# Rest-row query transposes in one group, W_out blocks fetched one product earlier in strip 0, and one tile's transposes later

## The chip, the cores and the metric

The kernel runs on one core of a Trainium2 chip. The metric is the device time of one execution in microseconds (us). Lower is better.

## The reference

Attention without softmax comes first, and a two-layer network on its output follows. All data are float32 in the kernel; the two weight matrices reach it as 64-bit floats and are converted on the chip.

```python
kv  = einsum('bhsd,bhse->bhde', k, v)      # q, k, v: 8 batches, 8 heads, 576 rows, 64 columns
out = einsum('bhsd,bhde->bhse', q, kv)
out = out / sqrt(mean(out*out, -1) + 1e-6) * g_norm
x   = out.transpose(0, 2, 1, 3).reshape(4608, 512)
h   = x @ w_in                             # 512 x 2048
y   = maximum(h, 0)**2 @ w_out             # 2048 x 512
```

## The kernel before

**Tiles and strips.** The 4608 rows of x form 36 tiles of 128 rows. Four tiles make a strip, so there are nine strips, 0 to 8. A batch has 576 = 4 x 128 + 64 rows. The 64 left over are the "rest" rows; those of an even batch and of the odd one after it share a tile (`k_rest`, `v_rest`, `q_rest`), so that two batches give nine tiles. Tile 8 is the last of batches 0 and 1, and the first that belongs to strip 2.

**Attention slices.** Attention is cut into a list `slices`. For each batch b and each pair of heads p there is `transposed_query(b, p)` and `key_value(b, p)`; after the four pairs of a batch come `query` and `normalized` for two tiles at a time, and a function that brings the normalized tile into the transposed form `xT` that the network needs: `features` (transposes on TensorE) for tiles of batches 0 and 1, `squares_x` (VectorE and DMA) afterwards. `attend(n)` runs the list up to place n. The main loop calls it between the products of the network, so the network's matmuls and attention share TensorE in one fixed order.

**Queries of batches 0 and 1.** They are transposed on TensorE into PSUM tile `t_ps` (L339) and copied out by ScalarE (L341). For odd b, that is b = 1 here, each pair of heads also transposes its part of `q_rest` (L345, PSUM tile `tr_ps`) and copies it (L348). `t_ps`, `kv_ps` of `key_value` (L357, copied by L359 and L360) and `xt_ps` of `features` (L475) take turns in two PSUM places (tag `at`, `bufs=2`). `tr_ps` uses the place of the query products `x_ps` (tag `x`, one place).

**Strip 0.** The up-products (L614) run while the weights are still being converted: ScalarE does L210 and L213 on a raw piece, VectorE L222 to L231, and SyncE loads the next piece into a freed place (L198). The down-products of strip 0 use one level of a Strassen-like scheme with seven products, in the order 1, 2, 5, 6, 7, 3, 4, each of 32 matmuls in two halves (L578). Products 1, 2 and 5 find their blocks of W_out in `w_in`'s place. Products 6, 7, 3 and 4 fetch theirs from a DRAM copy (`w_out`) with `stream()` into `w_blk` tiles.

**Blocks and their sums.** During the first half of each of the seven products VectorE also makes four sums of the product's block (`deep_sums`, 128 x 2048 in all, tile `w_t`). They are written to DRAM (`w_deep`, L698) for the later strips, which use two levels of the scheme (L768). `w_blk` and `w_t` share four places (tag `w_blk`). A new tile takes a place that has been freed and waits for the last use of it.

**Order.** Every engine executes its instructions in the order in which the program records them, and nothing is reordered by a scheduler. SyncE issues nearly all DMAs, so a DMA that waits holds the ones recorded behind it. `load_rest(2)` and `load_q_rest(2)` load the rest rows of batch 2; the second is eight small DMAs (L162). `sums_in(g)` (L257, L259, L248) scales and sums W_in's blocks for the later strips, and `sums_x(1)` makes four sums of strip 1's x for its products 5, 6, 7 and 4.

Of the kernel before, what the change touches and what calls it, by code (L numbers as in the profile page):

```python
# [10 lines left out]
FP32 = mybir.dt.float32  # L11
# [9 lines left out]
def kernel(  # L21
# [225 lines left out]
    def minus(eng, out, a, b):  # L247
        eng.tensor_tensor(out=out, in0=a, in1=b, op=ALU.subtract)  # L248
# [71 lines left out]
    def open_rest(b):  # L320
        t = qt_pool.tile([P, NP, P], FP32, name="qT_rest", tag="qT_rest", bufs=1)
        for p in range(NP):
            qT["rest", b // 2, p] = t[:, p]
        return t

    def transposed_query(b, p):
        t = main.pop(("q", b, p))
        if b >= Q_ON_PE:
            qT[b, p] = qt_pool.tile([P, C, P], FP32, name="qT", tag="qT")
            nc.vector.transpose(out=flat(qT[b, p]), in_=flat(t))  # L330
            if b % 2 and p == NP - 1:
                nc.vector.transpose(
                    out=open_rest(b).rearrange("p q (k t) -> p q k t", k=4),
                    in_=squares(q_rest[b // 2]).rearrange("p k q f -> p q k f"),
                )
            return
        ps = apsum.tile([P, C, P], FP32, name="t_ps", tag="at")
        for c in range(C):
            nc.tensor.transpose(ps[:, c, :], flat(t[:, c]), ident)  # L339
        qT[b, p] = qt_pool.tile([P, C, P], FP32, name="qT", tag="qT")  # L340
        nc.scalar.copy(qT[b, p], ps)  # L341
        if b % 2:
            t = q_rest[b // 2][:, 2 * p : 2 * p + 2]
            ps = apsum.tile([P, 2, C * P], FP32, name="tr_ps", tag="x", bufs=1)[:, 0, 0:P]
            nc.tensor.transpose(ps, flat(t), ident)  # L345
            if p == 0:
                open_rest(b)
            nc.scalar.copy(qT["rest", b // 2, p], ps)  # L348

    def key_value(b, p):  # L350
        tk, tv = main.pop(("k", b, p)), main.pop(("v", b, p))
# [168 lines left out]
    for b in range(1, B):  # L520
        for p in range(NP):
            slices += [(transposed_query, (b, p)), (key_value, (b, p))]
        first_n = b // 2 * PAIR + (C if b % 2 else 0)
        ns = list(range(first_n, first_n + C + b % 2))
        for i in range(0, len(ns), 2):
            slices += [(query, (ns[i : i + 2],)), (normalized, (ns[i : i + 2],))]
            for n in ns[i : i + 2]:
                slices.append((features if b < X_ON_PE else squares_x, (n,)))
                if n % NT == NT - 1:
                    ready[n // NT] = len(slices)  # L530
    slice_at = [0]

    def attend(n):
        while slice_at[0] < min(n, len(slices)):
            fn, a = slices[slice_at[0]]
            fn(*a)
            slice_at[0] += 1
# [115 lines left out]
    to_stream += [(s, p, n) for s in range(DEEP, N_STRIP) for p in DEEP_ORDER for n in range(2)]  # L653
    to_stream = iter(to_stream)

    def stream(n=1):
        for _, u in zip(range(n), to_stream):
            p = u[1]
            t = stream_pool.tile([P, 4, FQ // 2, P], FP32, name="w_blk", tag="w_blk")
            if len(u) == 2:  # L660
                w_blk[u] = t.rearrange("p (h a) f e -> p h (a f) e", h=2)
                nc.sync.dma_start(out=w_blk[u], in_=w_out[B_OUT[p]])
            elif u[2] == 0:

                nc.sync.dma_start(
                    out=t[:, 1:4], in_=w_out[B_OUT[p]].rearrange("p h (a f) e -> p (h a) f e", a=2)[:, 1:4]
                )
                for i, j in enumerate((3, 1, 2)):
                    w_blk[*u[:2], j] = t[:, i + 1]
            else:  # L670
                nc.sync.dma_start(out=t, in_=w_deep[B_OUT[p]])
                for i, j in enumerate((5, 6, 7, 4)):
                    w_blk[*u[:2], j] = t[:, i]
# [9 lines left out]
    def down(s, p, i):  # L683
        if i == 0:
            open_bank(p)
        a = {1: 11, 2: 21, 6: 11, 7: 12, 3: 21, 4: 22}.get(p)
        w = w_blk[s, p]
        product(
            p, i,
            lambda fc: (gq[s, 1, fc // 2][:, fc % 2] if p == 5 else gq[s, a][:, fc])[:, ts(i, P)],  # L690
            lambda fc: w[:, :, fc], FQ,
        )
        if i == 0:
            if s == DEEP - 1:
                deep_sums(p, w)
                if p == 2:
                    stream()
                nc.sync.dma_start(out=w_deep[B_OUT[p]], in_=deep.pop(p))  # L698
            return
        del w_blk[s, p]  # L700
        if p not in (1, 2):
            stream()
        if s == 0 and p in (1, 2, 5):

            for e in range(2):
                nc.sync.dma_start(out=w_out[B_OUT[p], :, e], in_=w_first[B_OUT[p]][:, :, ts(e, P)])

        if p == (1 if s else 2):
            for g in range(NG):
                x = gq[s, 11][:, ts(g, 2)]  # L710
                minus(nc.vector, x, gq[s, 1, g], x)
        if p == (2 if s else 5):
            minus(nc.vector, gq[s, 21], gq[s, 21], gq[s, 11])

        def store(th, eh):
            def f(b, a=None):
                o = out_tile()
                if a is None:
                    nc.scalar.copy(o, b)
                else:  # L720
                    nc.vector.tensor_tensor(out=o, in0=b, in1=a, op=ALU.add)
                send(s, th, eh, o)
            return f

        combine(p, store(0, 0), store(0, 1), store(1, 0), store(1, 1))
# [1 line left out]

    deep = {}

    def deep_sums(p, w):  # L730
        t = deep[p] = stream_pool.tile([P, 4, FQ // 2, P], FP32, name="w_t", tag="w_blk")
        b11, b12, b21, b22 = (w[:, e, ts(f, FQ // 2)] for f in range(2) for e in (1, 0))
        minus(nc.vector, t[:, 0], b12, b11)
        minus(nc.vector, t[:, 1], b22, t[:, 0])
        minus(nc.vector, t[:, 2], b22, b12)
        minus(nc.vector, t[:, 3], b21, t[:, 1])

    A_G = {4: 22, 1: 11, 2: 21, 6: 11, 5: 22, 7: 12, 3: 21}
    leaf, chain, part = {}, {}, {}
# [95 lines left out]
    for s in range(N_STRIP):  # L835
        attend(ready[s])
        if s == 0:
            steps = [(2, up_first, (g, fh, i)) for g in range(NG) for fh in range(2) for i in range(2)]
        else:
            steps = [(1, up, (s, g, p)) for g in range(NG) for p in ORDER]  # L840
        n_up = len(steps)
        if s < DEEP:

            steps += [(2, down, (s, p, i)) for p in (ORDER if s else (1, 2, 5, 6, 7, 3, 4)) for i in range(2)]
        else:
            steps += [(2, down_deep, (s, k, i)) for k in range(7) for i in range(2)]
        goal = ready.get(s + 1, len(slices))
        total, done = sum(w for w, _, _ in steps), 0
        for i, (w, fn, a) in enumerate(steps):
            if s == 0 and i < n_up:  # L850

                convert(5 + (3 * i + 2) // 4)
                if i in (5, 7, 9):
                    load_next()
                if i == 6:
                    load_q_rest(0, nc.sync)
                    load_rest(1, nc.sync)
                    load_q_rest(1, nc.sync)
            elif s == 0 and i == n_up:
                convert(len(conversions))  # L860
                conv.close()
                sum_pool = ctx.enter_context(tc.tile_pool(name="sum", bufs=8, reuse_waits="tile"))
                stream_pool = ctx.enter_context(tc.tile_pool(name="stream", bufs=4, reuse_waits="tile"))
            if s == 0 and n_up <= i < n_up + NG:
                sums_g(0, i - n_up)
            fn(*a)
            done += w
            if s:
                attend(ready[s] + int((goal - ready[s]) * min(done / (0.42 * total), 1)))
                if s >= DEEP and i == n_up - 3:  # L870
                    leaf_sums(s, 4)
                continue
            if i == n_up + 11:
                load_next()
            if i == n_up + 13:
                load_rest(2, nc.sync)
                load_q_rest(2, nc.sync)
            if i - n_up in (7, 9, 11, 13):
                sums_in((i - n_up - 7) // 2)
            if i == n_up + 11:  # L880
                sums_x(1)
            if i == len(steps) - 1:
                stream(2)

            n = i + 1 - (n_up - 6)
            pairs, m = divmod(max(n - 2 * NP, 0), 3)
            attend(min(ready[0] + min(max(n, 0), 2 * NP) + 4 * pairs + (0, 2, 2)[m], goal))


# [28 lines left out]
```

## Time and profile before

| | us |
|---|---|
| median of 4 runs | 939.78 |
| the runs | 936.84, 938.23, 941.33, 941.72 |
| the profiled execution | 938.23 |
| its span, first to last instruction | 936.1 |
| outside the span | 2.1 |
| TensorE busy / VectorE busy / ScalarE busy | 912.7 / 685.2 / 226.3 |

The engines are named PE (TensorE matmuls), PEld (TensorE weight loads), DVE (VectorE), ACT (ScalarE), POOL (GpSimd) and SP (SyncE); a q behind a name marks the engine's sequencer. L345 is line 345 of the kernel before. "out<-in" names the tile written and the tiles read. Times within the trace count from the first instruction.

### The profile page before, as it was taken

Reading aid. Unit: us, or ns where it says so; the run is one execution under the profiler, and the core shown is the slowest. Engines: PE = TensorE matmul, PEld = TensorE weight load, DVE = VectorE, ACT = ScalarE, POOL = GpSimd, SP = SyncE. Lnnn points to the kernel's source line nnn. Section 1 sums busy time; section 2 is a strip of 40 time slices with the busy share of each in tenths; the row PEclk is TensorE's granted clock in tenths of the full one; section 3 lists DMA queues with packets and bytes.
Section 4 is the critical chain, followed back from the end, with each engine's and each line's share of the span. In section 5 each row is a group of like instructions: output and inputs, shape, how many; then the busy total and the mean of one; then the engine's idle time right before and its main releaser. Section 6 shows DMA issues by size and latency. Waiting matters only on the chain.

```text
span 936.1 us, 17429 instructions
## 1 busy us (share of the span) xinstructions
PE 912.7 (97%) x7048; PEld 807.9 (86%) x7048; DVE 685.2 (73%) x1195; ACT 226.3 (24%) x497; POOL 1.7 (0%) x7
## 2 busy tenths in 40 slices
PE   5899999999999999999999999999999999999998
PEld 4444887889988998899889998899889988998898
DVE  3999887479846985589748974797559854983496
ACT  4797332230023002310221013201220022002200
POOL 0000000000000000000000000000000000000000
PEclk9899999999999999999999999999999999999999
DMA  9699988737853685558564865487507731682075
GB/s 284 229 301 313 323 297 290 205 98 266 303 151 99 214 315 165 121 185 302 190 147 145 301 228 144 104 286 247 174 26 252 283 99 57 240 288 69 0 265 174
DMA packets 165295, 191.46 MB, mean 205 GB/s; under 512 B 84064, under 2 KB 137824, under 8 KB 156640
## 3 DMA queue, kind: packets, MB, share of 16 engines
q1 hardware_dynamic: 164896, 190.23, 63.2%
q8 instruction: 55, 0.90, 0.4%
q10 hardware_dynamic: 320, 0.13, 0.1%
q14 instruction: 24, 0.20, 0.1%
HBM read 159.12 MB, written 31.20 MB: 203 GB/s over the span
## 4 chain that ended last, share of the span: by engine, by line
PE 87%; DVE 7%; DMA 3%; issue 1%; SPq 1%; ACT 1%; DVEq 0%; ACTq 0%
PE ps_A L578 24%; PE ps_B L768 21%; PE ps_A L768 16%; PE ps_B L578 13%; PE ps_C L578 6%; PE kv_ps L357 2%; PE x_ps L388 2%; DVE w_c L228 1%; DMA w_blk<-w_out 1%; DVE w_in L231 1%; PE ps_A L614 1%; PE ps_C L614 1%; DVE w_c L222 1%; DMA q_rest<-in_q_dram 1%; DMA raw<-in_moe_w_in_dram 1%
## 5 line engine op out<-in xcount | busy, mean ns | idle before, releaser
L578 PE MATMUL ps_A<-x_t,w_in 128*128 128x256 f32 x768 | 183.1, 381 | 0.0
L578 PEld LDWEIGHTS ps_A<-x_t,w_in 128*128 128x128 f32 x768 | 144.5, 190 | 20.0
L768 PE MATMUL ps_B<-w_blk,g_s 128*128 128x128 f32 x1024 | 124.8, 275 | 0.0
L768 PEld LDWEIGHTS ps_B<-w_blk,g_s 128*128 128x128 f32 x1024 | 119.5, 192 | 0.0
L768 PE MATMUL ps_B<-w_blk,gt 128*128 128x128 f32 x768 | 96.2, 275 | 0.0
L768 PE MATMUL ps_A<-w_blk,g_s 128*128 128x128 f32 x768 | 93.6, 275 | 0.0
L768 PEld LDWEIGHTS ps_B<-w_blk,gt 128*128 128x128 f32 x768 | 91.5, 192 | 0.4
L768 PEld LDWEIGHTS ps_A<-w_blk,g_s 128*128 128x128 f32 x768 | 89.6, 192 | 0.0
L637 DVE TENSOR_TENSOR gt<-ps_A,snap 128x512 f32<-128x512 f32 x32 | 22.1, 689 | 74.4 <-PE ps_A L578 74.4
L768 PE MATMUL ps_A<-w_blk,gt 128*128 128x128 f32 x576 | 72.2, 275 | 0.0
L638 DVE SCALAR_TENSOR_TENSOR gt<-gt 128x512 f32<-128x512 f32 x96 | 66.4, 692 | 3.3
L768 PEld LDWEIGHTS ps_A<-w_blk,gt 128*128 128x128 f32 x576 | 68.2, 192 | 0.0
L637 DVE TENSOR_TENSOR gt<-ps_C,snap 128x512 f32<-128x512 f32 x32 | 22.1, 690 | 62.3 <-PE ps_C L578 62.3
L588 ACT COPY snap<-ps_A 128x512 f32<-128x512 f32 x66 | 38.7, 586 | 117.0 <-PE ps_A L578 105.9
L578 PE MATMUL ps_A<-xT,w_in 128*128 128x256 f32 x256 | 61.3, 382 | 0.0
L578 PE MATMUL ps_C<-xT,w_in 128*128 128x256 f32 x256 | 61.1, 381 | 0.0
L578 PE MATMUL ps_B<-xT,w_in 128*128 128x256 f32 x256 | 61.0, 381 | 0.0
L578 PE MATMUL ps_B<-x_t,w_in 128*128 128x256 f32 x256 | 61.0, 381 | 0.0
L248 DVE TENSOR_TENSOR gt<-gt 128x2048 f32<-128x2048 f32 (+1 forms) x29 | 59.9, 2065 | 0.1
L782 DVE TENSOR_TENSOR o_sb<-o_sb,ps_B 128x256 f32<-128x256 f32 (+1 forms) x128 | 49.5, 386 | 12.1 <-ACT o_sb L783 4.2
L578 PEld LDWEIGHTS ps_B<-xT,w_in 128*128 128x128 f32 x256 | 48.2, 190 | 6.7
L578 PEld LDWEIGHTS ps_B<-x_t,w_in 128*128 128x128 f32 x256 | 48.2, 190 | 6.7
(118 smaller groups left out, 1108.5 us busy)
## 6 DMA issues: line engine op xcount, KB each, us to landing
w_blk<-w_deep SPq DMA_DIRECT2D x56, 1024.0 KB, 5.2
w_blk<-w_out SPq DMA_DIRECT2D x56, 768.0 KB, 5.0
raw<-in_moe_w_in_dram SPq DMA_DIRECT2D x16, 512.0 KB, 5.9
raw<-in_moe_w_out_dram SPq DMA_DIRECT2D x16, 512.0 KB, 5.1
k<-in_k_dram SPq DMA_DIRECT2D x29, 256.0 KB, 3.2
v<-in_v_dram SPq DMA_DIRECT2D x29, 256.0 KB, 3.6
w_deep<-w_t SPq DMA_DIRECT2D x7, 1024.0 KB, 5.2
x_d<-x_q SPq DMA_DIRECT2D x27, 256.0 KB, 2.1
```

The costliest lines, as they stand in the source:

```text
L222: yield nc.vector.tensor_scalar(out=c, in0=c, scalar1=LEAST, scalar2=MOST, op0=ALU.max, op1=ALU.min)
L228: yield nc.vector.scalar_tensor_tensor(out=ci, in0=high, scalar=-(2**30), in1=ci, op0=ALU.bitwise_and, op1=ALU.bitwise_or)
L248: eng.tensor_tensor(out=out, in0=a, in1=b, op=ALU.subtract)
L357: nc.tensor.matmul(ps[ts(h, D)], lhsT=a, rhs=w, start=c == 0, stop=c == C)
L388: nc.tensor.matmul(ps[half, r, i, ts(p, D)], lhsT=q[row, half], rhs=kvd[b, p][row, row], start=True, stop=True)
L578: nc.tensor.matmul(bank[BANK[p]][:, i, :], lhsT=lhsT(k), rhs=rhs(k), start=p in (1, 5, 2) and i == 0 and k == 0, stop=k == n - 1, skip_gro ...
L588: nc.scalar.copy(snap[p], b)
L614: nc.tensor.matmul(ps, lhsT=w_in[:, kc % KH, g, kc // KH * 2 + fh, ts(i, P)], rhs=xt[0][:, :, kc, :], start=kc == 0, stop=kc == NP - 1,)
L637: nc.vector.tensor_tensor(out=o, in0=b, in1=a, op=ALU.add)
L638: nc.vector.scalar_tensor_tensor(out=o, in0=o, scalar=0.0, in1=o, op0=ALU.max, op1=ALU.mult)
L768: nc.tensor.matmul(chain[c][x][:, i, :], lhsT=a[:, f, :], rhs=w[:, f, :], start=p not in (6, 7, 3) and j in ((1, 2) if place(s, p) is LAST ...
L782: add = lambda out, a, b: nc.vector.tensor_tensor(out=out, in0=a, in1=b, op=ALU.add)
```

## The change

It has four parts. All of them touch strip 0 and the first products of strip 1; from there on the recorded order of every engine is the same.

1. The four separate transposes of `q_rest` and their four copies become one slice, `rest_queries`, after the last `key_value` of batch 1: four transposes into one PSUM tile, and one copy of 128 x 512. `attend`'s goal counts the additional slice.
2. Each of the blocks for products 6, 7, 3 and 4 is fetched about one product earlier. The places for the sums of products 5, 7 and 4 are taken ahead (`reserve`), before the fetch that is recorded next. The sums of product 6 go to four small tiles of another pool and are written by four DMAs of 256 KB in place of one of 1 MB.
3. The transposes of tile 8 (`features(8)`) move from directly behind its normalization to behind `transposed_query(2, 0)` and `key_value(2, 0)`.
4. The loads of batch 2's rest rows are recorded after step 9 in place of step 13 of the down-products, ahead of the block for strip 1's first product and the keys, values and queries of batch 2's second pair.

```diff
@@ transposed_query
-        if b % 2:
-            t = q_rest[b // 2][:, 2 * p : 2 * p + 2]
-            ps = apsum.tile([P, 2, C * P], FP32, name="tr_ps", tag="x", bufs=1)[:, 0, 0:P]
-            nc.tensor.transpose(ps, flat(t), ident)
-            if p == 0:
-                open_rest(b)
-            nc.scalar.copy(qT["rest", b // 2, p], ps)
+    def rest_queries(b):
+        ps = apsum.tile([P, 2, C, P], FP32, name="tr_ps", tag="x", bufs=1)[:, 0]
+        for p in range(NP):
+            nc.tensor.transpose(ps[:, p], flat(q_rest[b // 2][:, 2 * p : 2 * p + 2]), ident)
+        nc.scalar.copy(open_rest(b), ps)
@@ the list of slices
             slices += [(transposed_query, (b, p)), (key_value, (b, p))]
+            if (b, p) == (X_ON_PE, 0):
+                slices += late
+        if b % 2 and b < Q_ON_PE:
+            slices.append((rest_queries, (b,)))
...
             for n in ns[i : i + 2]:
+                if b < X_ON_PE and i == C:
+                    late = [(features, (n,))]
+                    continue
                 slices.append((features if b < X_ON_PE else squares_x, (n,)))
@@ stream
+    def reserve(p):
+        deep[p] = stream_pool.tile([P, 4, FQ // 2, P], FP32, name="w_t", tag="w_blk")
@@ down
             if s == DEEP - 1:
-                deep_sums(p, w)
-                if p == 2:
-                    stream()
-                nc.sync.dma_start(out=w_deep[B_OUT[p]], in_=deep.pop(p))
+                if p == 6:
+                    parts = [sum_pool.tile([P, FQ // 2, P], FP32, name=f"w_t{i}", tag="sum") for i in range(4)]
+                    deep_sums(parts, w)
+                    for i, t in enumerate(parts):
+                        nc.sync.dma_start(out=w_deep[B_OUT[p], :, i], in_=t)
+                    return
+                if p not in deep:
+                    reserve(p)
+                t = deep.pop(p)
+                deep_sums([t[:, i] for i in range(4)], w)
+                nc.sync.dma_start(out=w_deep[B_OUT[p]], in_=t)
             return
         del w_blk[s, p]
-        if p not in (1, 2):
+        if s == 0 and p in (2, 6, 3):
+            reserve({2: 5, 6: 7, 3: 4}[p])
+        if p not in (1, 7):
             stream()
@@ main loop, strip 0
+            if i == n_up + 1:
+                stream()
             if i == n_up + 11:
                 load_next()
-            if i == n_up + 13:
+            if i == n_up + 9:
                 load_rest(2, nc.sync)
                 load_q_rest(2, nc.sync)
...
-            attend(min(ready[0] + min(max(n, 0), 2 * NP) + 4 * pairs + (0, 2, 2)[m], goal))
+            attend(min(ready[0] + min(max(n, 0), 2 * NP) + (n >= 2 * NP) + 4 * pairs + (0, 2, 2)[m], goal))
```

`deep_sums` does the same four subtractions as before, on the tiles that it is given.

More of the change, by code (lines that the diff above doesn't have):

```diff
@@ L728, with deep_sums @@
     deep = {}
-    def deep_sums(p, w):
-        t = deep[p] = stream_pool.tile([P, 4, FQ // 2, P], FP32, name="w_t", tag="w_blk")
+    def deep_sums(t, w):
         b11, b12, b21, b22 = (w[:, e, ts(f, FQ // 2)] for f in range(2) for e in (1, 0))
[L733 to L736, printed above, removed]
+        minus(nc.vector, t[0], b12, b11)
+        minus(nc.vector, t[1], b22, t[0])
+        minus(nc.vector, t[2], b22, b12)
+        minus(nc.vector, t[3], b21, t[1])
     A_G = {4: 22, 1: 11, 2: 21, 6: 11, 5: 22, 7: 12, 3: 21}
```

## The prediction

> **What bounds the kernel now.** I read the page's first part, then the busy time by stretches, PE's own waits, and the timelines of PE, ACT and SP around each wait.
>
> ```profile
> span 936.1 us, 17429 instructions
> PE 912.7 (97%) x7048; PEld 807.9 (86%) x7048; DVE 685.2 (73%) x1195; ACT 226.3 (24%) x497; POOL 1.7 (0%) x7
> ```
>
> PE is idle for 23.4 us of the span. The stretches (stretch, length, then busy us of PE, PEld, DVE, ACT, POOL, the granted clock, DMA share, GB/s) say where. 9.2 us lie in 0 to 20 and 5.3 us in 20 to 40, in code that the change leaves alone, and 4.3 us in the tail after 930. The other idle places before 205 us are these:
>
> ```profile
> 70.00:80.00 10.00, 8.10 (x41) 3.87 (x40) 10.00 (x24) 9.38 (x24) 0.00 (x0) 1.00 1.18 287
> ...
> 130.00:140.00 10.00, 9.27 (x44) 7.84 (x43) 8.98 (x14) 5.33 (x5) 0.00 (x0) 1.00 0.91 334
> 140.00:150.00 10.00, 9.65 (x45) 8.22 (x44) 7.83 (x14) 0.00 (x0) 0.00 (x0) 1.00 0.98 359
> 150.00:160.00 10.00, 9.21 (x71) 7.50 (x70) 7.84 (x16) 4.95 (x7) 0.00 (x0) 1.00 0.71 201
> 160.00:180.00 20.00, 19.15 (x138) 16.23 (x139) 8.16 (x13) 4.70 (x12) 0.00 (x0) 1.00 0.84 236
> ```
>
> That is 1.90 + 0.73 + 0.35 + 0.79 + 0.85 = 4.62 us. From 180 to 925 us PE is busy in every stretch without a gap, so a microsecond won before 180 us reaches the end whole, and nothing else can be won. PE's own waits (us in all, times, longest) name the same gaps:
>
> ```profile
> PE tr_ps L345 <- DMA q_rest<-in_q_dram: 1.9, 1, 1.9
> PE xt_ps L475 <- DVE x_n L429: 1.6, 1, 1.6
> ...
> PE ps_B L578 <- DMA w_blk<-w_out: 0.7, 1, 0.7
> PE ps_A L578 <- DMA w_blk<-w_out: 0.3, 1, 0.3
> ```
>
> So 4.6 us (0.5%) is about the ceiling, and the question is which waits take the place of those removed.
>
> **Part 1, the rest queries.** PE's timeline:
>
> ```profile
> 71.43 0.60 PE L339 MATMUL t_ps<-ident,q 128*128 128x128 f32 x4
> 73.93 0.30 PE L345 MATMUL tr_ps<-ident,q_rest 128*128 128x128 f32 x1 [1.90 <-DMA q_rest<-in_q_dram]
> ...
> 94.50 0.69 PE L357 MATMUL kv_ps<-more_qkv 128*64 128x64 f32 x16
> ```
>
> Transposes start 0.11 us apart (the second pair's L345 starts at 82.52, the next product at 82.63). Without L345 the product that started at 74.21 starts at 71.43 + 4 x 0.11, about 71.9: 2.3 us sooner. The L345s of the second and third pair save 0.11 each, so PE comes to `kv_ps` of the third pair at 94.50 - 2.5 = 92.0. On the way, `kv_ps` of the first pair wants rest rows of k and v issued at 66.20 and 67.06; with the 6.05 us that `q_rest` took they land by 73.1, for use at 75.5. The second pair's q is issued by 72.81 and takes 4.2 (the page's row of 128 KB q loads): 77.0, for use at 79.8. Both hold. What is late next is the PSUM place: `kv_ps` of the third pair takes the one that `kv_ps` of the second pair had, and ACT frees it:
>
> ```profile
> 89.10 0.68 ACT L210 ACTIVATE w_c<-raw 128x512 f32<-128x512 f32 x1 [3.75 <-DMA raw<-in_moe_w_out_dram]
> ...
> 93.25 0.19 ACT L359 COPY kv_all<-kv_ps 64x64 f32<-64x64 f32 x1
> 93.45 0.21 ACT L360 COPY kv_all<-kv_ps 64x64 f32<-64x64 f32 x1
> ```
>
> ACT runs in order, and ahead of these copies stand two conversions of raw pieces whose loads SP issued at 83.89 and 84.55, paced by DVE's conversions and not by PE. The copies therefore still end at 93.66, and PE now waits there from 92.0 to about 93.7: **a new wait of 1.7 us**, and a lead of 0.8. Bounds: 0 if the raw piece lands 0.8 later, 2.5 if ACT is not late; I take 0.8, the row itself. The fourth L345 gives 0.11 more. The four grouped transposes then cost 4 x 0.11, and 0.1 for the changeover, in front of product 2. Net at product 2: 0.8 + 0.1 - 0.5 = **0.4 us**. The one 128x512 copy (0.57 in L341's row; four of 0.27 go) follows two small copies on ACT and ends near 105; `x_ps`, which needs its place and its result, starts at 107.27. Costed at nothing.
>
> **Part 2, blocks one product sooner.** SP's timeline:
>
> ```profile
> 128.75 0.33 SPq L698 DMA_DIRECT2D w_deep<-w_t  x1
> 129.19 0.37 SPq L662 DMA_DIRECT2D w_blk<-w_out  x1
> 135.92 0.32 SPq L698 DMA_DIRECT2D w_deep<-w_t  x1
> 136.34 0.38 SPq L662 DMA_DIRECT2D w_blk<-w_out  x1
> ```
>
> The block for product 3 is issued at 129.19, behind the write of product 6's sums, which waits for DVE; it lands 7.58 us later (the chain of waits has this piece), and product 3 starts at 136.81 after waiting 0.73. Product 4's is the next pair of rows and costs 0.35. After the change they stand in the places of the blocks now issued at 120.44 and 129.19, so with 7.6 to 8.4 us (median 8.1 for these 1 MB fetches) they land near 128.5 and 137, for use near 136 and 143: 7 and 6 us of cover. **Gain 1.08 us.** If the cover went, the cost is the old waits. The other things behind it: three fetches now precede writes on a queue that is 0.88 to 1.06 busy from 100 to 150. The write of W_out's part for product 5 (issued at 120.92) must land before DVE overwrites that part at about 132. One more 1 MB at 300 GB/s is 3.5 us at most, if the queue had no free moment (share 0.88 in 110 to 120 says it has some: 1.2 us). DVE then has idle time of 2.0 (before 144.03) and 1.6 (before 154.04), and `sums_x`, done near 148.7 for product 6 of strip 1 at 155.49, has 3.6 us left after a lead of 3.2. Bounds 0 and 1; I take 0.
>
> The four 256 KB writes of product 6's sums stand ahead of product 4's block. The page gives 5.2 us to land 1 MB of sums, 3.2 for a 256 KB load of k: even if the four did not overlap, 12.8 against 5.2 is 7.6 later, which would take the 6 us of cover and 1.6 more. They are issued about 0.6 apart as DVE makes them, so I expect overlap and no cost. The Trainium skill speaks against the split: "DMA: Bandwidth & Descriptors", section Bandwidth, says to batch DMAs to 1 MiB or more for 75% of peak. By its fit of 2.0 us plus bytes at 436 GB/s (for the GpSimd path), four in a row would take an estimated 10.4 us against 4.4, and the gain of this part would still be whole; no row here shows such a split.
>
> **Part 3, tile 8.** PE waits 1.64 us at 160.85 for DVE's normalization, which ends at 160.8. After the change products 7 and 3, `kv_ps` of batch 2 and product 4 come first (1.73 + 1.73 + 0.73 + 1.73 = 5.9 us). With the lead of 1.5, PE passes the old place near 157.6 and needs tile 8 at 163.5: cover 2.7. Product 7 needs ACT's copy of bank A (157.52 + 0.59, itself moving with PE), in time as in later groups. **Gain 1.64 us.** The new `xT` copy on ACT is needed only in strip 2.
>
> **Part 4, the rest loads of batch 2.** Ten DMAs (157.93 to 164.95 on SP: 7.0 us) move ahead of the sums of product 3, a block, and the second pair's k, v and q. SP idles from 137.7 to 142.0, so these move back by some 2.7 us; k and v landed at about 153 and are used at 172.8. Behind them, k and v of the third pair (issued at 167.34 when `kv_ps` of batch 2 frees their place) gain: SP is free earlier there. Zero, with DVE's in-order `qT` transposes as the ones who would wait.
>
> **Sum.** 0.4 + 1.08 + 1.64 = 3.1, call it 3.2 with the changeovers saved. The profiled execution took 938.23 (span 936.1 and 2.1 around it): 935.0. It is 1.55 below the median of the runs, 939.78; against that, **936.6 us**.
>
> **The rivals.** *The whole ceiling, or more.* If ACT's copies come earlier, or if in the longer executions (941.33, 941.72) the blocks land later than in the profiled one (the block for product 7 landed within 0.4 us of its use), the change removes more: 4.6 to 7 us, 932.8 to 935.2. Against: the ACT rows above. *Given back.* The raw piece lands 0.8 us later, or the writes hold DVE at 132: parts 1 and 2 vanish, 1.6 or less remains: 938 to 940.5. *Slower.* SP is held by the read of `w_deep` for strip 1 (it waited 3.8 us at 157.06 for its write), and the keys and values of batch 2's third pair stand behind it. Before, v landed 1.0 us ahead of its use at 177.1. It is slower by over 0.5% once they land 3.2 + 4.7 + 1.0 = 8.9 us later relative to PE, say 945. For it: a write that shares the queue with earlier fetches. Against: eight small loads no longer stand between. *Nothing done*, because a fetch still waits for its place: the recorded waits speak against it.
>
> **How the numbers follow.** Forecast 0.52 (935.3 to 938.0), ceiling or more 0.30, given back 0.12, slower 0.06. About 0.5% is what a measurement of this kernel can tell from no change: below 935.1 or above 944.5. Faster 0.30 + 0.04 of the forecast's edge = 0.34; slower 0.06; the rest 0.60. The range 933.0 to 940.5 leaves out the slower case and the ends of two others.
>
> **What would show it.** Right: PE waits at `kv_ps` of batch 1's third pair near 92 to 94 us for ACT's L360, 1.2 to 2.2 us long; no PE wait for `w_blk`, `q_rest` or tile 8's `x_n`; strip 1's first product near 149.8 instead of 151.32. Wrong: no wait near 92 (part 1 then gives 2.1), or a PE gap between 165 and 180.

## The result, and the profile after

| | before | after |
|---|---|---|
| median, us | 940.32 (77 runs) | 937.45 (49 runs) |
| lowest to highest | 936.84 to 943.77 | 932.32 to 941.42 |
| ratio of the times, 95% interval | | 0.9969, 0.9961 to 0.9977 |
| the profiled execution / its span | 938.23 / 936.1 | 938.90 / 937.1 |

The change saves 2.9 us (2.2 to 3.7 by the interval) where 3.2 were forecast. The profiled execution of the changed kernel is one of its longer ones, so its lines do not show the gain. They show best what the change did to each wait. The page's head and TensorE's own waits (us in all, times, longest; those of the start-up left out):

```profile
span 937.1 us, 17433 instructions
PE 912.3 (97%) x7048; PEld 809.1 (86%) x7048; DVE 685.1 (73%) x1195; ACT 226.0 (24%) x494; POOL 1.7 (0%) x7
```

```profile
PE kv_ps L355 <- ACT kv_all L358: 6.1, 1, 6.1
...
PE t_ps L339 <- ACT qT L341: 0.7, 1, 0.7
```

The waits for `q_rest`, for both blocks `w_blk` and for tile 8's `x_n`, 4.62 us together, are gone. In their place stands one wait for ScalarE (L355, L357 and L358 are the old L357, L359 and L360), and a small one ahead of it. The busy time by stretches:

```profile
80.00:90.00 10.00, 9.34 (x43) 4.31 (x42) 9.63 (x25) 4.45 (x9) 0.00 (x0) 1.00 1.01 317
90.00:100.00 10.00, 3.94 (x27) 2.62 (x26) 6.16 (x16) 6.87 (x18) 0.00 (x0) 0.72 1.04 304
100.00:110.00 10.00, 10.00 (x65) 8.51 (x64) 8.28 (x16) 3.09 (x9) 0.00 (x0) 0.94 0.96 286
130.00:140.00 10.00, 10.00 (x52) 8.83 (x51) 6.99 (x12) 7.08 (x6) 0.00 (x0) 1.00 1.05 345
...
160.00:180.00 20.00, 20.00 (x143) 16.91 (x142) 9.57 (x19) 6.09 (x15) 0.00 (x0) 1.00 0.85 275
```

TensorE now has no idle time from 130 us on. Between the start-up and that point all of its idle time, 0.66 + 6.06 us, lies between 80 and 100, and the mean granted clock is 0.72 in the second of these stretches. TensorE's timeline shows both:

```profile
87.54 3.60 PE L620 MATMUL ps_C<-xT,w_in 128*128 128x512 f32 x8
97.19 1.12 PE L355 MATMUL kv_ps<-more_qkv 128*64 128x64 f32 x16 [6.05 <-ACT kv_all L358]
...
98.45 5.04 PE L584 MATMUL ps_A<-w_in,gt 128*128 128x256 f32 x16
```

The half product at 98.45 takes 5.04 us. The same 16 matmuls take 3.72 at the full clock. ScalarE's timeline tells what it did until 97:

```profile
92.58 0.66 ACT L210 ACTIVATE w_c<-raw 128x512 f32<-128x512 f32 x1 [5.59 <-DMA raw<-in_moe_w_out_dram]
93.15 0.67 ACT L213 ACTIVATE raw<-raw 128x512 int32<-128x512 uint32 x1
94.17 0.66 ACT L210 ACTIVATE w_c<-raw 128x512 f32<-128x512 f32 x1 [0.36 <-DMA raw<-in_moe_w_out_dram]
...
96.73 0.19 ACT L357 COPY kv_all<-kv_ps 64x64 f32<-64x64 f32 x1
96.93 0.21 ACT L358 COPY kv_all<-kv_ps 64x64 f32<-64x64 f32 x1
```

It idled 5.59 us for the second-to-last raw piece of W_out, with the copies that TensorE needs queued behind it. That is the wait that the prediction named, in its place, but 6.1 us long and not 1.7.

The rest of the kernel passes a shift on whole. From strip 1's first two-level product to the end of the span it is 726.8 to 727.1 us in all 14 profiled executions. What differs between executions is when the transposes of batch 1's first pair start (67.8 to 71.4 us), and the stretch from there to that product, called *the stretch* below: 137.65 us in the profiled execution before, 140.63 after.

### The profile page after: what moved, and what is told of

The parts are those of the page before. It is cut to its first block, busy times and chain, and to the rows that moved or that the text cites. A ratio compares the mean times of both kernels' runs of the same rounds, so it can differ in the third digit from the quotient of the medians.

```text
span 937.1 us, 17433 instructions
## 1 busy us (share of the span) xinstructions
PE 912.3 (97%) x7048; PEld 809.1 (86%) x7048; DVE 685.1 (73%) x1195; ACT 226.0 (24%) x494; POOL 1.7 (0%) x7
## 4 chain that ended last, share of the span: by engine, by line
PE 89%; DVE 5%; DMA 3%; issue 1%; ACT 1%; SPq 0%; DVEq 0%; ACTq 0%
PE ps_A L584 27%; PE ps_B L787 21%; PE ps_A L787 16%; PE ps_B L584 13%; PE ps_C L584 7%; PE kv_ps L355 2%; PE x_ps L386 2%; DVE w_c L228 2%; DMA raw<-in_moe_w_out_dram 1%; DVE w_c L222 1%; DVE w_in L231 1%; DMA q_rest<-in_q_dram 1%; DMA raw<-in_moe_w_in_dram 1%; DMA k_rest<-in_k_dram 0%; DVE wt L248 0%
## 5 line engine op out<-in xcount | busy, mean ns | idle before, releaser
L787 PE MATMUL ps_B<-w_blk,gt 128*128 128x128 f32 x768 | 96.2, 275 | 0.0
L787 PE MATMUL ps_A<-w_blk,g_s 128*128 128x128 f32 x768 | 93.6, 275 | 0.0
```

The costliest lines, as they stand in the source:

```text
L787: nc.tensor.matmul(chain[c][x][:, i, :], lhsT=a[:, f, :], rhs=w[:, f, :], start=p not in (6, 7, 3) and j in ((1, 2) if place(s, p) is LAST ...
```

## Experiments

Theory S says that part 1's lead is taken back by ScalarE's copies, which stand behind the last raw pieces. Ratios are to the kernel before, run on the same chip. R1 to R12 name the kernels of the experiments; the number of runs of each is given. The lines shown are of one profiled execution of each.

**R1. Part 1 alone** (12 runs).

```diff
  kernel before, and
-        if b % 2: ...                 # the four separate transposes and copies
+    def rest_queries(b): ...          # four transposes, one copy
...
+        if b % 2 and b < Q_ON_PE: slices.append((rest_queries, (b,)))
```

> Part 1 alone (the four transposes of q_rest in one group), all else as before. Theory S (the lead is taken back by ACT's copies behind the raw pieces): the wait for q_rest (1.9 us) is gone, PE waits 1.5 to 6 us at kv_ps of batch 1's third pair instead, later as the last raw pieces land later; the waits for w_blk and tile 8 stay. Time 0 to 0.8 us under before, ratio 0.999 to 1.000; if the raw pieces land late, no better than before. Rival R (the removed wait counts whole): no wait at kv_ps, 2.3 us under before, ratio 0.9975.

Measured 942.05 us, ratio 1.0017 (0.9996 to 1.0038): about 1.6 us slower, if anything, where theory S had 0.999 to 1.000. TensorE's waits:

```profile
PE kv_ps L356 <- ACT kv_all L359: 4.4, 1, 4.4
...
PE ps_B L579 <- DMA w_blk<-w_out: 1.4, 1, 1.4
...
PE ps_A L579 <- DMA w_blk<-w_out: 0.9, 1, 0.9
```

The wait for `q_rest` is gone, and one of 4.4 us stands at `kv_ps`, with the clock at half from 94.85 to 98.26 us behind it.

**R2. Part 2 alone** (12 runs).

```diff
  kernel before, and
+    reserve(p), the four small tiles for product 6's sums, and stream() one product sooner
```

> Part 2 alone (blocks of W_out one product sooner, places reserved, sums of product 6 in four tiles). Theory S: both waits for w_blk go, nothing takes their place but up to 0.3 us at tile 8; the wait for q_rest stays. 1.1 to 1.5 us under before, ratio 0.9985. Rival: the blocks land later than in the trace of before in most executions, so more is won, 2 us or over, ratio 0.998 or lower. Rival: the four small writes hold product 4's block, ratio 1.000 and a wait for w_blk at product 4.

Measured 937.63 us, ratio 0.9972 (0.9959 to 0.9984): 2.6 us saved, where the prediction had 1.1. That is the sign of the first rival, that the blocks land later in most executions than in the profile before. No wait for a block is left. The other two stay:

```profile
PE tr_ps L345 <- DMA q_rest<-in_q_dram: 3.4, 1, 3.4
...
PE xt_ps L475 <- DVE x_n L429: 1.6, 1, 1.6
```

**R3. The changed kernel without part 4** (12 runs).

```diff
-            if i == n_up + 9:
+            if i == n_up + 13:
                 load_rest(2, nc.sync)
```

> The changed kernel with part 4 undone: batch 2's rest rows are loaded after step 13 again. Theory S: with PE some 3 us earlier than before, key_value of batch 2 comes before its rest rows have landed (before: landed at 163.9 and 164.6, used at 166.6), so a new wait of 1 to 3 us for k_rest or v_rest at kv_ps near 164; 1 to 3 us over the changed kernel, ratio to before 0.998 to 1.000. Rival (part 4 costs and gains nothing, as the prediction had it): same as the changed kernel, 0.997.

Measured 942.30 us, ratio 1.0019 (0.9999 to 1.0038), about 4.7 us above the changed kernel's 0.9969. The profiled execution, 945.87 us, is one of its longest. SyncE's timeline and TensorE's wait:

```profile
157.15 1.15 SPq L715 DMA_DIRECT2D w_deep<-w_t  x1
162.55 0.34 SPq L680 DMA_DIRECT2D w_blk<-w_deep  x1
162.98 0.39 SPq L690 DMA_DIRECT2D out_dram<-o_sb  x1
163.42 0.64 SPq L148 DMA_DIRECT2D k_rest<-in_k_dram  x1
164.11 1.19 SPq L148 DMA_DIRECT2D v_rest<-in_v_dram  x1
```

```profile
170.28 0.48 PE L355 MATMUL kv_ps<-v_rest,k_rest 128*64 128x64 f32 x4 [3.74 <-DMA v_rest<-in_v_dram]
```

SyncE stands still from 158.3 to 162.55, because the read of `w_deep` waits for its write. The rest rows of batch 2 are recorded behind that read, and TensorE waits 3.74 us for them. In the changed kernel they are issued ahead of it:

```profile
142.79 1.22 SPq L148 DMA_DIRECT2D k_rest<-in_k_dram  x1
144.06 1.13 SPq L148 DMA_DIRECT2D v_rest<-in_v_dram  x1
```

**R4. The changed kernel with the last raw pieces loaded first** (6 runs).

```diff
  load_more:
             load_piece()
+            if len(raw) == len(sources):
+                load_next()               # batch 1's fourth pair, after the last pieces
  key_value:
-            if b == 1 and p < 2:
+            if b == 1 and p == 1:
                 load_next()
```

> The changed kernel with one swap on SP: the last two raw pieces are issued ahead of k, v and q of batch 1's fourth pair in place of behind them. Theory S (the wait at kv_ps of the third pair hangs on the landing of these pieces): they land some 3.7 us earlier relative to PE, the wait shrinks from 6.05 us (changed kernel's trace) to under 2.5, or to none where the pieces were not late, and the granted clock stays at full speed in 90 to 100 us; 1 to 5 us under the changed kernel, ratio to before 0.992 to 0.996. What is late next is g_s of product 5 (0.7 us). Rival (the wait belongs to that one execution, or ACT is late for another reason): same as the changed kernel, 0.997.

Measured 935.28 us, ratio 0.9943 (0.9920 to 0.9965). In this execution the last piece was issued at 82.11 and landed at 88.61, and of TensorE's waits these are left:

```profile
PE ps_B L586 <- DVE g_s L613: 1.0, 1, 1.0
...
PE kv_ps L357 <- ACT kv_all L360: 0.3, 1, 0.3
```

The wait hangs on the landing, as theory S says. R10 and R11 show how far that carries.

**R5. The changed kernel with ScalarE's conversion later** (7 runs).

```diff
-        for i in range(acted[0], min(ids[-1] + 3, len(sources))):
+        ahead = 1 if ids[-1] == len(sources) - 3 else 3
+        for i in range(acted[0], min(ids[-1] + ahead, len(sources))):
```

> Edit: in the changed kernel ScalarE's conversion of the last pair of raw pieces is recorded one conversion step later, that is behind the copies of kv_ps and gt instead of ahead of them; the loads of these pieces stay where they are. Theory S (the lead of part 1 is taken back because ScalarE's copies stand in order behind the last raw pieces): TensorE's wait of 6.1 us at kv_ps and the half clock behind it go or fall under 1 us although the pieces land as late as before, the span is near 932 and the ratio to the kernel before near 0.994, as with the raw pieces loaded first. Rival (it is the queue: whatever loads last at 85 to 95 us lands late, and VectorE, which converts these pieces too, then holds the products of strip 0): the wait at kv_ps is replaced by one on VectorE's w_c or g_s of 3 us or more, ratio 0.997 or above.

Measured 937.76 us, ratio 0.9957 (0.9939 to 0.9976). The wait at `kv_ps` for ScalarE is gone. The rival's sign is there as well:

```profile
110.58 2.75 PE L585 MATMUL ps_B<-w_in,g_s 128*128 128x256 f32 x12
116.45 2.07 PE L585 MATMUL ps_B<-w_in,g_s 128*128 128x256 f32 x4 [3.12 <-DVE g_s L612]
```

Product 5 waits 3.12 us for its sums `g_s` from VectorE. The span is 937.1 us in this execution, R5's longest, and not theory S's 932, and the ratio cannot tell this kernel from the changed one.

**R6. Both cures** (6 runs): R4's and R5's edits in the changed kernel.

> Edit: the changed kernel with both cures, the last two raw pieces loaded ahead of the fourth pair's k, v and q, and ScalarE's conversion of them one step later. Theory S: the two cures remove the same wait, of which loading first left 0.3 us, so the ratio is that of loading first, 0.994 within 0.001. Rival (loading first gains in other ways, and ScalarE's order costs on top of it): ratio 0.992 or below.

Measured 935.53 us, ratio 0.9948 (0.9933 to 0.9963), as for R4. The profile has a wait of 4.1 us for `g_s`.

**R7. The raw pieces first in the kernel before** (11 runs): R4's edit alone.

> Edit: the kernel before, with only the last two raw pieces loaded ahead of the fourth pair's k, v and q. Theory S: in the kernel before TensorE comes to kv_ps later than ScalarE's copies, so there is nothing to cure: ratio 1.000 within 0.001. Rival (in most executions of the kernel before these pieces land late too, and their late landing costs it time of its own): ratio 0.998 or below, and then part of the gain of loading first isn't owed to the change.

Measured 940.30 us, ratio 0.9999 (0.9986 to 1.0012). There was nothing to cure there.

**R10. Part 1 alone with the raw pieces first** (12 runs): R1's and R4's edits.

> Edit: the kernel before with part 1 alone, and the last two raw pieces loaded ahead of the fourth pair's k, v and q. Part 1 alone measured 1.0017, loading first alone 0.9999. Theory S: with the raw pieces early, the lead of part 1 survives the copies of kv_ps: TensorE waits there under 1 us, without half clock, and the ratio is 0.998 or below (2.3 us of lead, less what waits for the blocks). Rival (the lead is lost anyway, to the blocks of W_out, whose waits were 2.3 us in the run with part 1 alone): the w_blk waits grow to 3 us or more and the ratio stays at 0.999 or above.

Measured 940.18 us, ratio 0.9993 (0.9978 to 1.0008). Theory S's number does not come, and the wait that it had under 1 us is 3.7:

```profile
PE kv_ps L358 <- ACT kv_all L361: 3.7, 1, 3.7
...
PE ps_A L581 <- DMA w_blk<-w_out: 1.4, 1, 1.4
PE ps_B L581 <- DMA w_blk<-w_out: 1.3, 1, 1.3
```

The last pieces were issued at 82.16 and 84.55 and took 7.9 and 8.0 us to land (5.7 and 6.5 in R4). Issuing them first did not bring them in first. The blocks took 2.7 us, a little below the rival's 3.

**R8. Parts 3 and 4 alone** (12 runs).

```diff
  kernel before, and
+            if (b, p) == (X_ON_PE, 0):
+                slices += late
...
+                if b < X_ON_PE and i == C:
+                    late = [(features, (n,))]
+                    continue
...
-            if i == n_up + 13:
+            if i == n_up + 9:
                 load_rest(2, nc.sync)
```

> Edit: the kernel before with parts 3 and 4 alone (tile 8's transposes later, the loads of batch 2's rest rows earlier). The prediction gave part 3 1.6 us and part 4 nothing: ratio 0.9983, no wait of TensorE for tile 8's x_n, and none for k_rest or v_rest of batch 2. Rival (part 4 has a price of its own: ten loads ahead of strip 1's first block and of the second pair's keys make one of these late): a wait of 1 us or more between 150 and 180 us for w_blk, k or v, ratio 1.000 or above.

Measured 938.93 us, ratio 0.9985 (0.9968 to 1.0003), close to the 0.9983 expected, though the interval just reaches no change. The waits for tile 8 and for `v_rest` at 160 to 180 us are absent.

**R9. The changed kernel without part 1** (9 runs): R1's edit taken out again. **R11.** R4's kernel again (10 runs), and **R12.** the changed kernel itself (9 runs), all on one chip.

> Edit: the changed kernel with part 1 undone (the transposes of q_rest and their copies back in transposed_query), parts 2 to 4 kept. Theory A (part 1 alone cost 1.6 us because it trades the short wait for q_rest for a longer one on ScalarE, and the parts add up): without it the kernel is faster than the changed one, about 0.9969 x 0.9985 / 1.0005 = 0.995 to 0.996 of the kernel before; TensorE waits 2 to 3.5 us for q_rest near 73, 0 to 2 us at kv_ps near 95, and for no block and no tile 8. Rival (the prediction's: part 1 gains 0.4 us): ratio 0.997 or above, slower than the changed kernel.

> The changed kernel with the last two raw pieces loaded ahead of the fourth pair's k, v and q, on the same chip as the changed kernel itself. Theory S: 0.9943 was no accident of few runs: 0.994 to 0.996, and 1 to 3 us faster than the changed kernel beside it. Rival: no more than 0.5 us between the two.

> The changed kernel as it is, beside the two kernels derived from it on the same chip. Theory S: a wait of 1.7 us or more at kv_ps near 90 to 98 us with ScalarE as its releaser, as long as the landing of the last raw pieces makes it, and half clock behind it where it is over 3 us; ratio 0.996 to 0.998. Rival: a profile without this wait at the same time.

| on one chip | median, us | ratio | interval |
|---|---|---|---|
| R9, without part 1 | 935.18 | 0.9949 | 0.9929 to 0.9970 |
| R11, raw pieces first | 936.18 | 0.9956 | 0.9940 to 0.9971 |
| R12, the changed kernel | 936.72 | 0.9952 | 0.9932 to 0.9972 |

The three cannot be told apart. R11's median is 0.5 us below R12's, which is the rival's number, and by the ratios it is the other way round, so R4's advantage over the changed kernel is not confirmed. R11's profile has the wait again:

```profile
PE kv_ps L357 <- ACT kv_all L360: 3.5, 1, 3.5
```

The last piece was issued at 82.09, as early as in R4, but the copies end at 92.94 and not at 91.70, TensorE was ready 2.0 us sooner, and the clock was at half from 94.1 to 97.5 us. When that piece landed is not recorded. Loading first was run three times with part 1 and ScalarE's order as it was, in R4, R10 and R11, and the profile lacks a long wait in R4 alone.

R9 came out where theory A (part 1 alone loses) put it against the kernel before, but that it is faster than the changed kernel is not shown either. Part 1 brings nothing that these runs can see. R12's ratio is below the 0.996 to 0.998 expected, into which its interval reaches. R9's lines and R12's:

```profile
95.68 0.69 PE L357 MATMUL kv_ps<-more_qkv 128*64 128x64 f32 x16 [1.50 <-ACT kv_all L360]
...
175.61 0.69 PE L357 MATMUL kv_ps<-v,k 128*64 128x64 f32 x16 [0.82 <-DMA v<-in_v_dram]
```

```profile
93.96 0.69 PE L355 MATMUL kv_ps<-more_qkv 128*64 128x64 f32 x16 [3.69 <-ACT kv_all L358]
...
94.69 3.72 PE L584 MATMUL ps_A<-w_in,gt 128*128 128x256 f32 x16
```

R9 waits 2.6 us for `q_rest` and then 1.50 here. R12 waits 3.69 here, without the half clock that its expectation had behind a wait of over 3 us. R12's execution took 934.63 us. Its stretch is 136.25 us, 4.4 below the one shown first: 3.0 of it is the shorter wait at `kv_ps` and the absent one of 0.66 us ahead of it, 0.4 goes back to another small wait, and 1.8 is the half clock that it was spared.

**What the set shows.** The end of ScalarE's copies follows the landing of the last raw piece by the same time in each execution that has ScalarE's order unchanged and the landing recorded:

| | last piece issued, landed | copies end | after landing | TensorE's wait |
|---|---|---|---|---|
| before | 84.55, 90.58 | 93.66 | 3.08 | 0 |
| R1 | 84.78, 90.93 | 93.98 | 3.05 | 4.4 |
| R2 | 84.42, 92.23 | 95.31 | 3.08 | 0 |
| R3 | 86.70, 94.57 | 97.62 | 3.05 | 6.0 |
| R4 | 82.11, 88.61 | 91.70 | 3.09 | 0.3 |
| R7 | 82.23, 88.49 | 91.58 | 3.09 | 0 |
| R8 | 83.05, 88.89 | 91.98 | 3.09 | 0 |
| R10 | 84.55, 92.53 | 95.58 | 3.05 | 3.7 |
| R9 | 84.31, 92.56 | 95.63 | 3.07 | 1.5 |
| R12 | 84.62, 90.86 | 93.91 | 3.05 | 3.7 |
| after | 86.35, 94.09 | 97.14 | 3.05 | 6.1 |

With part 1 TensorE is ready for `kv_ps` at 89.7 to 91.9 us, and without it at 93.6 to 96.2. In both cases it goes on at the landing plus 3.1 or at its own readiness, whichever is later. The piece takes 5.8 to 8.3 us to land after its issue, and 6.0 to 8.3 where SyncE issued it within 0.5 us of the same time (before, R1, R2, R9, R12). So part 1 can win no more than what the copies leave to spare without it: 0.8 us before, 0.9 in R2, 1.6 in R8 and 2.7 in R7. In R9 they left nothing. The second barrier follows. In R4, R5, R6, R10 and R12 VectorE starts the last of product 5's sums 7.8 us after the one before it, in one chain behind a wait of 2.0 to 3.1 us for the write of the converted pieces (`w_out<-wt`). In R12 the matmuls ahead of that use end at 111.66 + 2.75 = 114.41, and the sums are done at 114.16, only 0.25 us sooner. R5 and R6, which open the first barrier, run into it.

So the gain of the change comes from parts 2 to 4: R9 has these alone, and beside the changed kernel it measured the same.

What stays open: by how much part 1 alone loses (the interval of R1 runs from 0.4 us gained to 3.6 lost), why the same piece lands up to 2 us later in one execution than in another, and whether any of R4, R6 or R9 beats the changed kernel. No version here is shown to.

## Why the prediction was right, and where not

The time fell inside the range, and the sum of 3.2 us is close to the measured 2.9. That it came out is in part luck, since two terms were off in opposite directions. Taken alone, the parts measured +1.6 (R1), -2.6 (R2) and -1.4 us (R8), together -2.4, against -0.4, -1.08 and -1.64 predicted. Part 1 shows no gain, and part 2 gained more than twice its term.

- **Part 1, predicted 0.4 us gained.** The mechanism was right to the line: a new wait at `kv_ps` of batch 1's third pair, for ScalarE's second copy, behind the last two conversions. Its size was not: 6.1 us in the profile after, 3.7 in R12, 4.4 in R1, against 1.7. The step that failed is the term of 0.8 ("I take 0.8, the row itself"): it took one execution's landing of the last piece for all. Of the eleven flights above, the 6.0 us that the term rested on is the second shortest. In the profile after the piece landed 3.5 us later than before: 1.8 by its issue (a load of k at 72.8 us held SyncE for 1.65 us in place of 0.62, among others) and 1.7 by its own time in flight. A late landing alone would still leave the term at its lower bound, 0, because TensorE would then go on at the landing plus 3.1 with part 1 and without it. Below that lies the half clock behind the longer wait (next point), and perhaps a later issue: with the old order of these loads the last piece was issued at 84.62 to 86.70 us in the five profiles with part 1 (after, R1, R3, R5, R12) and at 83.05 to 84.55 in the four without (before, R2, R8, R9). That part 1 causes this is not shown. With ScalarE's order unchanged, TensorE goes on at `kv_ps` at 94.7 us on average in the seven profiles with part 1, and at 94.9 in the five without: on this average nothing of the 2.5 us of lead was left there.
- **What a long wait adds.** The prediction costed idle time only. Behind the 6.05 us the clock was at half from 94.3 to 101.2 us, which stretched the `kv_ps` group from 0.73 to 1.26 us and the half product from 3.72 to 5.04: 1.85 us more. Of the 50 runs of the changed kernel with a recorded mean clock (the profiled one among them), 25 are at 0.993 or less, at 938.4 us on average, and the other 25 average 936.6. Of 80 such runs of the kernel before, 16 are. This agrees, but a run's mean clock does not tell where it was lost. The old wait could lose it too: behind R2's 3.4 us for `q_rest` the clock was at half from 74.4 to 77.8 us.
- **Part 2, predicted 1.08.** The waits went as said. The term was sized by one execution, in which they were 1.08 us. In the other profiles with the old order of blocks they were 2.3 (R1), 2.3 (R7), 0.7 (R8) and 2.7 (R10). The mean of the five is 1.8, inside R2's interval (1.5 to 3.9 us). The prediction had this case, under its first rival, as blocks that land later in the longer executions. It belonged in the forecast.
- **The four 256 KB writes, predicted free.** They landed 4.4 to 6.8 us after their issue and overlapped: the last three were issued from 134.59 on and were all in 5.7 us later, where one after another they would have taken 4.4 + 5.0 + 4.7 = 14.1. Product 4's block, issued behind them at 136.04, landed at 143.07, 4.4 us ahead of its use at 147.47. The Trainium skill speaks against such a split ("DMA: Bandwidth & Descriptors", section Bandwidth: batch DMAs to 1 MiB or more). In this place the split made TensorE wait for no block.
- **Part 3, predicted 1.64.** The wait is absent in every kernel with it. R8's 1.4 us agrees, within a wide interval.
- **Part 4, predicted zero.** It has a use and a small price. The use: R3 shows that parts 2 and 3 live on it. There the rest loads were issued 5.5 us later than in the profile before (163.42 against 157.93), while TensorE came to their use at 166.5 us (167.1 before), so at their old place they cost 3.7 us of waiting and some clock. The prediction saw the read of `w_deep` holding SyncE, only for another load and with the sign of a rival. The cover of part 3 ended at these loads. The price: v of batch 2's third pair takes 8.7 to 11.0 us to land in the eight profiles with part 4 and 6.3 to 8.3 in the six without, R3 among them with 7.2. The prediction had this load gain. In the profile after it landed 0.4 us ahead of its use (1.0 before), and in R4, R9 and R11 TensorE waited 0.57, 0.82 and 0.85 us for it.
- **The point named as a sign.** Strip 1's first product was to start near 149.8. It started at 154.38 in the profile after and at 149.37 in R12. A single profile could have called it either way. The sign against it, a gap between 165 and 180 us, is absent in the profile after and there in R4, R9 and R11 (for v) and in R12 (0.43 us, for VectorE).

Of the rivals, the first was right that all 4.62 us would go, and wrong that nothing would come in their place. The second, *given back*, happened to part 1 alone. The slower case did not occur, but its path is the one that shows in R4, R9 and R11, at under 1 us.

## What to carry to other kernels

When a wait of TensorE is removed, look for the next event that does not move with TensorE (here a load paced by VectorE and by SyncE's queue), and cost the lead up to that event and no further, with the spread of its landing taken from all loads of its kind, and with what a longer wait costs in clock below zero. Size a wait for a DMA from several executions: one profile gave 1.1 us where the mean was 1.8. And where a change makes one engine arrive sooner, find the loads whose slack it uses up or that its own loads push back; moving them can look free and be what holds the gain.

## What the runs showed of the hardware

The half clock follows a grid, not the length of a wait. In the records of every profile the clock changes at steps of 3.41 us. Laying this grid over TensorE's idle time between 60 and 200 us, the clock was at half in the next step whenever 2.01 us or more of a step were idle (eleven steps, 2.01 to 3.41 us) and never from the full clock where 1.94 us or less were. In the start-up, before 60 us, the line is less sharp: five steps with 1.82 to 1.98 us idle lost the clock, and one with 1.91 us kept it. So R5's wait of 3.12 us lost the clock with 2.03 us of it in one step, and R12's of 3.69 us did not, split by the grid into 1.93 and 1.76. The Trainium skill ("TensorE: Matmul & The Clock Gate", section "What's actually happening") states a free-running window of 3413 ns, and the grid agrees. It also states that the clock is throttled after at least one idle window; that is more than these runs show, as 53 to 60% of one was enough.
